# Linear attention and an ELU feed-forward layer: the second layer by seven products on all of K, exp and relu in place in G, and work placed anew on the engines

## The chip, the cores and the metric

The kernel runs on one core of a Trainium2 chip. A core has five engines that the profile names: PE (TensorE, matrix products; PEld is its loading of weights), DVE (VectorE), ACT (ScalarE), POOL (GpSimd) and SP (SyncE, which only issues DMA transfers here). The metric is the time of one execution in microseconds on the device; the time given is the median of several runs.

## The reference, cut to what matters

```python
# q, k, v: [batch 8, heads 8, seq 576, head_dim 64], f32
q_s = softmax(q, over head_dim)
k_s = softmax(k, over seq)
kv = np.einsum('bhsd,bhse->bhde', k_s, v)
attn = np.einsum('bhsd,bhde->bhse', q_s, kv)
x = attn.transpose(0, 2, 1, 3).reshape(4608, 512)
h = x @ w_in                                  # [4608, 512] @ [512, 2048]
g = np.where(h > 0, h, np.exp(np.minimum(h, 0)) - 1)
out = g @ w_out                               # [4608, 2048] @ [2048, 512]
```

## The kernel before

**Tiling.** The attention is worked in sixteen units n, one for each batch and half of its heads (two pairs of heads). A unit's q, k and v are loaded (L359); ScalarE takes the exponentials of q (L398, L428) and k (L402); VectorE sums q's over head_dim (L430) and takes the reciprocal (L433); QS (L441) is the scaled q; v is cast to bf16 in VB (L418), with a column of ones for k's sums. TensorE or a DMA transposes QS (L465, L481), TensorE makes kv (L521), VectorE or ScalarE writes it to MBLK (L530, L534), TensorE makes attn (L552, L564), and copies (L586 on ScalarE, L589 on VectorE) bring it into XT, the ring of transposed x.

The feed-forward part goes over nine blocks j of 512 tokens. The first layer of a block has eight groups g. A group (`hg_mm`, L637) is eight 128x512 matmuls, into one of the four PSUM slots of 1024 columns (blocks 2 to 8 take turns between two). Then `hg` takes exp on ScalarE (L653) into ESB, relu(1 - exp) on ScalarE in ESB (L673), and two operations of VectorE, max(h, 0) minus that, into G (L676). The even groups of blocks 0 and 1 have two operations of VectorE instead (L681, L683). G (tile GR) has 24 units of 512 columns, written and read in turn; a block fills sixteen.

The second layer reads G. K, 2048 long, is sixteen tiles of 128, in eight pairs z, which three groups hold: z 0 to 3, 4 and 5, 6 and 7. The plain way (`out_mm`, L698) takes sixteen 128x512 matmuls for 128 tokens. The other way (`pair`) works on 256 tokens, half of a block, and is a form of Strassen's method after Winograd: per z seven products of 256 columns (`mms`, L850) in the place of four of 512. It needs sums of G's quarters A11, A12, A21, A22 (`sums` and `late`, by `add_sum`, L798): four for each group of z in each pair, in place in G or into SB. It needs differences of the weights' quarters (`combos`, L769), made once, and additions of the partial results out of PSUM (`dve`, L871), with two copies for each pair (`copy`, L876). NSP = 6 holds room for six z only: blocks 2 to 5 do z 6 and 7 plainly (`std`, L863), and from block 6 on (WHOLE) TB2 and SB2, which lie where q and k were loaded before, serve the third group. Blocks 0 and 1 are plain throughout.

**What sets the order.** Each call of `S.add` records an operation with its engine, a cost and what it reads, writes or alters (R, W, X). ORDER is a list of operation numbers for each engine, written out: an engine issues in exactly that order, and `emit` puts a semaphore wait where an operation depends on another engine's. Costs, due times and DMA rates in `Sched` serve only to model the start of each operation; from it `fill` takes the number of spare matmuls (L956) that keep TensorE busy ahead of the first real ones. An operation that waits holds all that stand behind it in its engine's list. Loads are issued from SP's and GpSimd's queues (L359; W1 at L379 and W2 at L388 from GpSimd's), output stores from SP's (L731).

Of the kernel before, what the change touches and what calls it, by code (L numbers as in the profile page):

```python
# [21 lines left out]
NSP = 6  # L22
# [26 lines left out]
    "act": (  # L49
# [12 lines left out]
    "dve": (  # L62
# [35 lines left out]
}  # L98


class Op:
    __slots__ = ("eng", "dur", "emit", "deps", "key", "idx", "start", "end",
                 "dma", "sem", "val", "clock", "nbytes", "follow", "side", "late", "packet", "margin",
                 "gate", "span", "behind", "early")

    def __init__(self, eng, dur, emit, key, dma=None, nbytes=0):
        self.eng, self.dur, self.emit, self.key = eng, dur, emit, key
        self.deps = {}
        self.dma, self.nbytes = dma, nbytes
        self.start = self.end = None  # L110
        self.behind, self.early = None, 0
        self.follow, self.side, self.packet, self.margin = None, 0, 4608, 0


class Sched:
# [4 lines left out]
    LAND = 350  # L120
# [40 lines left out]
    def order(self):  # L161
# [4 lines left out]
        while any(line.values()):  # L166
            before = len(seq)
            for e in self.ENG:
                while line[e]:
                    o = line[e][0]  # L170
                    near = [d for d in (o.follow, o.gate, o.behind) if d is not None]
                    if any(d.end is None for d in list(o.deps) + near):
                        break
# [982 lines left out]
```

## Time and profile before

| what | us |
| --- | --- |
| median of three runs | 294.91 (294.35 to 295.12) |
| span of the profiled execution | 292.2 |
| clearing, loads and transposes up to the first matmul of the first layer | 14.27 |
| end of block 0's first layer | 29.91 |
| last sixteen first-layer matmuls of the last block end | 273.4 |
| idle time of VectorE ahead of L676, waiting for relu | 55.0 in 46 waits |
| idle time of ScalarE ahead of exp (L653), waiting for matmuls | 36.9 in 43 waits |
| idle time of GpSimd ahead of v casts (L418), waiting for loads | 16.1 in 5 waits |

The span is one execution as the profiler recorded it, from the first instruction to the last; the runs' times hold something more ahead and behind. In the lines of the profile, L637 is a line of the kernel, `x8` a count, `GR<-PS,ESB` reads "writes GR, reads PSUM and ESB", and the shapes are partitions x elements. "Busy" is the time that an engine is at work on instructions; the chain of waits is followed back from the last instruction to what released it at each step. The clock granted to TensorE is full in the whole span.

### The profile page before, as it was taken

What the parts mean: (1) busy time and instruction counts of PE and PEld (TensorE: products, weight loads), DVE (VectorE), ACT (ScalarE), POOL (GpSimd) and SP (SyncE); (2) the same over time, 40 slices, a digit from 0 to 9 for tenths busy, and PEclk for the clock granted to TensorE, in tenths of its full rate; (3) what the DMA queues carried; (4) which work ended last, traced back from release to release, by engine and by line L of the source; (5) the groups of instructions that cost most, each with busy time, mean ns of one, the idle gap of its engine ahead of it and who ended that gap; (6) DMA issues with size and microseconds to landing.
All of it is one profiled execution on the core that took longest, in us unless ns stands there. A gap on an engine that the chain in (4) does not pass through costs nothing.

```text
span 292.2 us, 5351 instructions
## 1 busy us (share of the span) xinstructions
PE 282.1 (97%) x2128; PEld 242.1 (83%) x2128; DVE 177.4 (61%) x326; ACT 211.3 (72%) x249; POOL 220.6 (76%) x216
## 2 busy tenths in 40 slices
PE   2899999999999999999999999999999999999994
PEld 0478887778888888888988888988989889988994
DVE  3748834787464686575656675756542667356753
ACT  4858849988998989786976779856883667665610
POOL 1992435617788999899786979799678968899880
PEclk9999999999999999999999999999999999999999
DMA  7999999799995679577919476403111010400235
GB/s 254 397 367 388 389 389 335 169 281 332 274 316 125 101 232 159 168 182 254 234 45 207 150 157 202 98 16 77 38 36 36 2 31 5 110 0 2 55 90 144
DMA packets 36472, 50.01 MB, mean 171 GB/s; under 512 B 16352, under 2 KB 18144, under 8 KB 36448
## 3 DMA queue, kind: packets, MB, share of 16 engines
q1 hardware_dynamic: 29680, 33.96, 43.5%
q0 software_dynamic: 6528, 15.47, 17.6%
q10 hardware_dynamic: 240, 0.26, 0.4%
q8 instruction: 16, 0.26, 0.4%
q14 instruction: 8, 0.07, 0.1%
HBM read 36.70 MB, written 9.44 MB: 158 GB/s over the span
## 4 chain that ended last, share of the span: by engine, by line
PE 94%; DMA 2%; POOL 2%; SPq 0%; issue 0%; DVE 0%
PE PS L637 46%; PE PS L850 28%; PE PS L698 10%; PE PS L863 5%; PE PS L552 3%; DMA KR<-in_k_dram 2%; PE PS L521 2%; POOL W L379 1%; POOL VB L418 0%; PE PS L465 0%; POOL QS L441 0%; SPq L359 0%; PE PS L564 0%; DVE OSB L871 0%
## 5 line engine op out<-in xcount | busy, mean ns | idle before, releaser
L637 PE MATMUL PS<-XT,W 128*128 128x512 f32 x576 | 142.7, 393 | 0.1
L676 DVE SCALAR_TENSOR_TENSOR GR<-PS,ESB 128x512 fp32r<-128x512 f32 (+1 forms) x124 | 87.5, 705 | 59.6 <-ACT ESB L673 55.7
L637 PEld LDWEIGHTS PS<-XT,W 128*128 128x128 f32 x576 | 105.0, 188 | 21.5 <-DMA W<-in_moe_w_in_dram 0.5
L653 ACT ACTIVATE ESB<-PS 128x1024 f32<-128x1024 f32 x72 | 73.5, 1025 | 38.4 <-PE PS L637 36.9
L673 ACT ACTIVATE ESB<-ESB 128x1024 f32<-128x1024 f32 x64 | 67.8, 1060 | 1.5
L798 POOL TENSOR_TENSOR GR<-GR 128x512 fp32r<-128x512 f32 (+1 forms) x65 | 62.7, 982 | 5.5 <-PE PS L850 4.9
L871 DVE TENSOR_TENSOR OSB<-OSB,PS 128x256 f32<-128x256 f32 x84 | 34.6, 417 | 26.9 <-PE PS L850 25.7
L850 PE MATMUL PS<-W,GR 128*128 128x256 f32 x288 | 45.5, 284 | 0.0
L850 PE MATMUL PS<-TB,GR 128*128 128x256 f32 x288 | 43.8, 283 | 0.0
L441 POOL TENSOR_TENSOR QS<-QR,RZQ 128x1152 f16<-128x1152 f32 (+1 forms) x16 | 30.2, 1886 | 17.2 <-DVE RZQ L433 16.5
L850 PEld LDWEIGHTS PS<-W,GR 128*128 128x128 f32 x288 | 40.8, 190 | 2.0
L850 PEld LDWEIGHTS PS<-TB,GR 128*128 128x128 f32 x288 | 39.9, 191 | 1.7
L798 POOL TENSOR_TENSOR SB<-GR 128x256 fp32r<-128x256 f32 (+1 forms) x31 | 30.0, 973 | 11.4 <-DVE GR L676 10.4
L698 PE MATMUL PS<-W,GR 128*128 128x512 f32 x128 | 32.4, 395 | 0.0
L798 POOL TENSOR_TENSOR GR<-SB,GR 128x256 fp32r<-128x256 f32 (+1 forms) x31 | 29.9, 978 | 2.4 <-PE PS L850 1.9
L418 POOL CAST VB<-VR 128x1152 bf16<-128x1152 f32 (+1 forms) x16 | 17.7, 1106 | 16.1 <-DMA VR<-in_v_dram 16.1
L698 PEld LDWEIGHTS PS<-W,GR 128*128 128x128 f32 x128 | 23.4, 188 | 4.7 <-DVE GR L683 0.2
L430 DVE TENSOR_REDUCE ZQ<-QR 128x18 f32<-128x1152 f32 (+2 forms) x18 | 21.8, 1209 | 6.5 <-ACT QR L428 4.9
L586 ACT ACTIVATE XT<-PS 128x512 fp32r<-128x512 f32 (+6 forms) x32 | 19.2, 603 | 6.8 <-PE PS L552 3.0
L876 ACT ACTIVATE OSB<-PS 128x256 f32<-128x256 f32 x28 | 10.4, 377 | 18.3 <-PE PS L850 9.3
L402 ACT ACTIVATE KR<-KR 128x1152 bf16<-128x1152 f32 x16 | 18.4, 1157 | 0.8 <-DMA KR<-in_k_dram 0.8
L398 ACT ACTIVATE QR<-QR 128x1152 f32<-128x1152 f32 x14 | 16.3, 1161 | 1.5 <-DMA QR<-in_q_dram 1.5
(57 smaller groups left out, 220.4 us busy)
## 6 DMA issues: line engine op xcount, KB each, us to landing
out_dram<-OSB SPq DMA_DIRECT2D x61, 128.0 KB, 2.4
QR<-in_q_dram SPq DMA_DIRECT2D x12, 576.0 KB, 5.0
KR<-in_k_dram SPq DMA_DIRECT2D x12, 576.0 KB, 6.1
VR<-in_v_dram SPq DMA_DIRECT2D x12, 576.0 KB, 5.4
W<-in_moe_w_out_dram POOLq DMA_DIRECT2D x4, 1024.0 KB, 16.6
QR<-in_q_dram POOLq DMA_DIRECT2D x4, 576.0 KB, 12.1
VR<-in_v_dram POOLq DMA_DIRECT2D x4, 576.0 KB, 13.0
KR<-in_k_dram POOLq DMA_DIRECT2D x4, 576.0 KB, 11.1
```

The costliest lines, as they stand in the source:

```text
L402: S.add("act", t_act(1152, False), lambda e: e.activation(ek[:, :, :, :].rearrange("p h c d -> p (h c d)"), flat(k), AF.Exp), key - 2, X=[ ...
L430: S.add("dve", t_dve(m), lambda e, qp=qp, zp=zp: e.tensor_reduce(zp, qp, AX.X, ALU.add), key - 3, R=[f"qR{i}{x}" for x in xs], W=[f"ZQ{i}{ ...
L441: lambda e, qp=q[:, :, a:b, :], rz=rz, dst=qs[:, :, a:b, :]: e.tensor_tensor(dst, qp, rz, ALU.mult),
L586: S.add("act", t_act((h1 - h0) * n_, True), lambda e, dst=dst, src=src: e.activation(dst, src, AF.Copy), key, W=W, X=X)
L637: last = e.matmul(P[:, t * 512:(t + 1) * 512], self.W1[:, kc, tt * 128:(tt + 1) * 128], self.XT[:, kc, rc:rc + BLK], start=(kc == 0), stop ...
L653: S.add("act", t_act(1024, True), lambda e: e.activation(esb[:, :], self.PS[ps][:, :], AF.Exp), key, W=[f"E{i}"], X=banks)
L673: S.add("act", t_act(1024, False), lambda e: e.activation(esb[:, :], esb[:, :], AF.Relu, bias=1.0, scale=-1.0), key, X=[f"E{i}"])
L676: S.add("dve", t_dve(512 if j else 1024), lambda e, u=u: e.scalar_tensor_tensor(*(x[:, :, u, :] if j else x for x in (gt, P)), 0.0, ev[:, ...
L698: last = e.matmul(dst, self.tile(jb, jj, ts), self.W2[:, jj, c0:c1], start=(jj == 0), stop=(jj == 15))
L798: lambda e: e.tensor_tensor(dst, a, b, op), key, R=R, W=W, X=X, after=after)
L850: last = e.matmul(dst, a[i][:, y_, :], b[i][:, y_, :], start=start and i == 0 and y_ == 0, stop=stop and i == len(grps) - 1 and y_ == z - ...
L871: S.add("dve", t_dve(256), lambda e: e.tensor_tensor(dst, a, b, ALU.add), key, R=R, W=W, X=X, after=after)
```

## The change

- NSP goes from 6 to 8, so that TB and SB have room for all K. Every pair takes all three groups; `std`, TB2 and SB2 are gone. T1 of the third group lies in W2 like the others.
- The later half of block 1 (two of its four pieces of 128 tokens) goes by `pair(1, 1)`, placed beside the first layer of block 2; `combos` for all three groups come ahead of it.
- ESB is gone. exp, relu and the even groups' first operation write G itself, through GE, a second name of the same memory in f32; L676's successor works on it in place.
- For casts of v, QS, the copies out of PSUM, the widening copies, the combos and the sums, the caller gives the engines that can do it, each with its cost, and `add` takes the one in whose list of ORDER the operation stands. ORDER is new on all engines. By it VectorE makes 80 sums (3 before) and GpSimd 100 (133 before), VectorE 15 of the 30 copies of 256 columns, most copies into XT, 4 of 12 combos; ScalarE 7 of the 14 full v casts.
- Instructions: TensorE 2201 (2128), of these 96 of the second layer with 512 columns (192) and 840 with 256 (672); VectorE 446 (326), ScalarE 228 (252), GpSimd 171 (216). There are 13 spare matmuls (12).
- In the new order VectorE's first q sum stands ahead of the clearing of the identity matrix, on which the spare matmuls depend, and GpSimd issues W1's third and fourth pieces behind a cast of v, a load of q and a QS. W1's groups 4 and 5 come with one load in the place of two.
- The planner's own fields (follow, gate, margin, late) are gone and its constants changed.

```diff
--- before.py
+++ after.py
-NSP = 6
+NSP = 8
...
         self.ops = []
+        self.home = {int(i): e for e, line in ORDER.items() for i in line.split()}
...
+    def add(self, eng, dur, emit, key, R=(), W=(), X=(), dma=None, nbytes=0, after=(), side=0):
+        alts = eng if isinstance(eng, dict) else {}
+        if alts:
+            eng = self.home.get(len(self.ops))
+            eng = eng if eng in alts else next(iter(alts))
+            dur = alts[eng]
         op = Op(eng, dur, emit, key, dma, nbytes)
...
+    def copy(self, e, dst, src):
+        return e.activation(dst, src, AF.Copy) if e is self.nc.scalar else e.tensor_copy(dst, src)
...
+        self.GE = nc.alloc_sbuf_tensor_at("GE", [128, 24, 2, 256], F32, offset=nc.sbuf_base - 49152)
...
-        self.ESB = [a(f"ESB{i}", [128, 1024], F32) for i in range(2)]
         self.RAW = [{t: a(f"{t.upper()}R{i}", [128, 2, CH, D], F32) for t in "qk"}
         self.VR = a("VR0", [128, 2, CH, D], F32)
-        self.TB2 = nc.alloc_sbuf_tensor_at("TB2", [128, 4, 2, 256], F32R, offset=rbase)
-        self.SB2 = nc.alloc_sbuf_tensor_at("SB2", [128, 2, 128], F32R, offset=rbase + 8192)
...
+                cost = {"act": t_act(int(576 * (h1 - h0)), False), "gp": 77 + 488 * (h1 - h0)}
...
+                cost = {"gp": m * 2.0 + 30, "dve": t_dve(m)}
+                if n in self.BYPOOL and ys == [0]:
+                    cost = {"dve": t_dve(m), "gp": m * 2.0 + 30}
                 rz = self.RZQ[i][:, :, a:b].unsqueeze(3).broadcast_to([128, 2, b - a, D])
-                S.add(eng, m * 2.0 + 30 if eng == "gp" else t_dve(m),
+                S.add(cost, None,
...
+            cost = {"act": t_act((h1 - h0) * n_, True), "dve": t_dve((h1 - h0) * n_)}
+            S.add(dict(sorted(cost.items(), reverse=e_ == "dve")), None,
+                  lambda e, dst=dst, src=src: self.copy(e, dst, src), key, W=W, X=X)
...
-        i = self.eslot % len(self.ESB)
-        self.eslot += 1
-        esb = self.ESB[i]
-        S.add("act", t_act(1024, True), lambda e: e.activation(esb[:, :], self.PS[ps][:, :], AF.Exp), key,
-              W=[f"E{i}"], X=banks)
         us = [self.unit(j, g, tp) for tp in range(2)]
         gw = sum((self.gnames(j, tp, (g,)) for tp in range(2)), [])
-        if j == 1:
-            gw += sorted(set(sum((self.early(u) for u in us), [])))
-        gt = self.GR[:, us[0]:us[1] + 1:us[1] - us[0], :, :]
+        over = sorted(set(sum((self.early(u) for u in us), []))) if j == 1 else []
+        gt, ge = [x[:, us[0]:us[1] + 1:us[1] - us[0], :, :] for x in (self.GR, self.GE)]
         if j:
-            gt = gt.rearrange("p u c t -> p c u t")
+            gt, ge = [x.rearrange("p u c t -> p c u t") for x in (gt, ge)]
             P = P[:, :].rearrange("p (c u t) -> p c u t", c=2, u=2)
-            ev = esb[:, :].rearrange("p (c u t) -> p c u t", c=2, u=2)
         else:
-            gt, P, ev = gt.rearrange("p u c t -> p (u c t)"), P[:, :], esb[:, :]
...
+            gt, ge = [x.rearrange("p u c t -> p (u c t)") for x in (gt, ge)]
+            P = P[:, :]
+        S.add("act", t_act(1024, True), lambda e: e.activation(ge, P, AF.Exp), key, W=gw + over, X=banks)
+        if how == "a":
             S.add("act", t_act(1024, False), lambda e: e.activation(
-                esb[:, :], esb[:, :], AF.Relu, bias=1.0, scale=-1.0), key, X=[f"E{i}"])
+                ge, ge, AF.Relu, bias=1.0, scale=-1.0), key, X=gw)
             for u in range(2) if j else (slice(0, 2),):
                 S.add("dve", t_dve(512 if j else 1024), lambda e, u=u: e.scalar_tensor_tensor(
-                    *(x[:, :, u, :] if j else x for x in (gt, P)), 0.0, ev[:, :, u, :] if j else ev, ALU.max, ALU.subtract), key,
-                    R=[f"E{i}"], W=self.gnames(j, u, (g,)) + (sorted(set(self.early(us[u]))) if j == 1 else []) if j else gw,
-                    X=banks)
+                    *(x[:, :, u, :] if j else x for x in (gt, P)), 0.0, ge[:, :, u, :] if j else ge,
+                    ALU.max, ALU.subtract), key, X=(self.gnames(j, u, (g,)) if j else gw) + banks)
         else:
             S.add("dve", t_dve(1024, 2), lambda e: e.tensor_scalar(
-                esb[:, :], esb[:, :], 1.0, -1.0, ALU.min, ALU.add), key, X=[f"E{i}"])
+                ge, ge, 1.0, -1.0, ALU.min, ALU.add), key, X=gw)
             S.add("dve", t_dve(1024), lambda e: e.tensor_tensor(
-                gt, ev, P, ALU.max), key,
-                R=[f"E{i}"], W=gw, X=banks)
+                gt, ge, P, ALU.max), key, X=gw + banks)
...
+        S.add({"act": t_act(512, True), "dve": t_dve(512)}, None, lambda e: self.copy(e, osb[:, :], src), key,
+              W=[f"O{i}L", f"O{i}R"], X=[f"b{bk}"])
...
-        if grp == 2:
-            T2, T3, T4, T1 = [self.TB2[:, s, :, :] for s in range(4)]
-        else:
-            z0, z1 = GROUPS[grp]
-            (T2, T3, T4), T1 = [self.TB[:, s, z0:z1, :] for s in range(3)], B12
+        z0, z1 = GROUPS[grp]
+        (T2, T3, T4), T1 = [self.TB[:, s, z0:z1, :] for s in range(3)], B12
...
-    def groups(self, j):
-        return (0, 1, 2) if j >= WHOLE else (0, 1)
+        early = [f"Ox{i}{x}" for i in range(z0 // 2, z1 // 2) for x in "LR"]
+        for s, (dst, a, b, W, R) in enumerate((
+                (T3, B22, B12, [f"T1{grp}"], self.w2(grp)),
+                (T1, B12, B11, [f"T3{grp}"] + self.w2(grp), []),
+                (T2, B22, T1, [f"T0{grp}"] + early, [f"T3{grp}"]),
+                (T4, B21, T2, [f"T2{grp}"], [f"T0{grp}"]))):
+            n_ = (z1 - z0) * 256
+            S.add({"gp": n_ * 2.34 + 30, "dve": t_dve(n_)}, None, lambda e, dst=dst, a=a, b=b: e.tensor_tensor(
+                dst, a, b, ALU.subtract), key, R=R, W=W, after=S.ops[-1:] if s == 1 else ())
...
-    def add_sum(self, grp, dst, a, b, op, key, R, W, X, after, eng="gp"):
+    def add_sum(self, grp, dst, a, b, op, key, R, W, X, after):
         z0, z1 = GROUPS[grp]
         n_ = (z1 - z0) * 128
-        self.S.add(eng, n_ * 2.4 + 60 if eng == "gp" else t_dve(n_),
+        self.S.add({"gp": n_ * 2.4 + 60, "dve": t_dve(n_)}, None,
                    lambda e: e.tensor_tensor(dst, a, b, op), key, R=R, W=W, X=X, after=after)
         return self.S.ops[-1]
...
-            self.add_sum(grp, A12, A12, A11, ALU.subtract, key, m, [], n, [],
-                         "dve" if (j, ts) == (NBLK - 1, 1) else "gp")
+            self.add_sum(grp, A12, A12, A11, ALU.subtract, key, m, [], n, [])
...
         S = self.S
         end = (j, ts) == (NBLK - 1, 1)
-        grps = self.groups(j)
-        full = 2 in grps
-        b0, b1 = (6, 7) if ts and full else (4, 5)
+        grps, tail = (0, 1, 2), j >= WHOLE
+        b0, b1 = (6, 7) if ts and tail else (4, 5)
         H = [self.bank(b)[:, c:c + 256] for c in (0, 256) for b in (b0, b1)]
-        if full:
+        if tail:
             x, y, over = 2 * ts, 2 * ts + 1, []
...
-        def std(p, jj0, jj1, stop):
...
         def copy(dst, src, W, bk):
-            S.add("act", t_act(256, True), lambda e: e.activation(dst, src, AF.Copy), key, W=W,
+            S.add({"act": t_act(256, True), "dve": t_dve(256)}, None, lambda e: self.copy(e, dst, src), key, W=W,
                   X=[f"b{bk}"])
...
         def second():
-            if not full:
-                std(0, 2 * NSP, 16, False)
+            pass
...
         def fourth():
-            if not full:
-                std(1, 2 * NSP, 16, False)
-            elif not end:
+            if not end:
                 dve(XR, XR, H[3], [], [], [f"O{x}R", f"b{b1}"])
             mms(1, H[1], A22, T4, g, 2, stop=True)
             dve(XL, XL, H[1], [], [], [f"O{x}L", f"b{b1}"])
-            if not full:
-                dve(XR, XR, H[3], [], [], [f"O{x}R", f"b{b1}"])
...
-        for g0, g1 in ((3, 4), (4, 5), (5, 6), (6, 8)):
+        for g0, g1 in ((3, 4), (4, 6), (6, 8)):
             self.load_w1(g0, g1, range(4), -30)
...
         work = [(1, ts, 4 + ts, 12, 16) for ts in range(2)]
-        for jj in (0, 8):
-            work += [(1, ts, 4 + ts % 2, jj, jj + 8) for ts in range(2, 4)]
         for j in range(2, NBLK):
             for g in range(8):
                 self.hg(j, g, g % 2, key, "a")
                 paced(8 * j + g)
                 if j == 2:
-                    if g in (1, 2, 3, 4, 5, 7):
+                    if g in (0, 1):
                         w = work.pop(0)
                         self.out_mm(*w, key)
-                        if w[4] == 16:
-                            self.out_store(w[0], w[1], w[2], key + 1)
+                        self.out_store(w[0], w[1], w[2], key + 1)
+                    if g == 1:
+                        for grp in range(3):
+                            self.combos(key, grp)
+                        self.sums(1, 1, key, (0, 1, 2))
+                        parts = self.pair(1, 1, key)
+                    if g in (3, 4, 5, 6):
+                        parts[g - 3]()
                     if g == 7:
-                        self.combos(key, 0)
-                        self.combos(key, 1)
                         self.sums(2, 0, key, (0, 1))
                 else:
                     ts, i = g // 4, g % 4
-                    if g == 0 and j - 1 >= WHOLE:
-                        if j - 1 == WHOLE:
-                            self.combos(key, 2)
+                    if g == 0:
                         self.sums(j - 1, 0, key, (2,))
                     if i == 0:
                         parts = self.pair(j - 1, ts, key)
                     parts[i]()
                     if i == 1:
                         n_ = (j - 1 + ts, 1 - ts)
-                        self.sums(*n_, key, self.groups(j - 1) if ts == 0 else (0, 1))
+                        self.sums(*n_, key, (0, 1, 2) if ts == 0 else (0, 1))
```

More of the change, by code (lines that the diff above doesn't have):

```diff
@@ L102 @@
     __slots__ = ("eng", "dur", "emit", "deps", "key", "idx", "start", "end",
-                 "dma", "sem", "val", "clock", "nbytes", "follow", "side", "late", "packet", "margin",
-                 "gate", "span", "behind", "early")
+                 "dma", "sem", "val", "clock", "nbytes", "side", "early", "alts")
     def __init__(self, eng, dur, emit, key, dma=None, nbytes=0):
@@ L110, in __init__ @@
         self.start = self.end = None
-        self.behind, self.early = None, 0
-        self.follow, self.side, self.packet, self.margin = None, 0, 4608, 0
+        self.side = self.early = 0
 class Sched:
@@ L163, in order @@
         free = {e: 740.0 for e in self.ENG}
-        queue = {e: 0.0 for e in self.ENG}
-        seq = []
+        queue, seq = 0.0, []
         while any(line.values()):
-            before = len(seq)
+            ready = []
             for e in self.ENG:
-                while line[e]:
+                if line[e] and all(d.end is not None for d in line[e][0].deps):
                     o = line[e][0]
-                    near = [d for d in (o.follow, o.gate, o.behind) if d is not None]
-                    if any(d.end is None for d in list(o.deps) + near):
-                        break
-                    t = max([free[e]] + [d.end + self.hop(d, o) for d in o.deps] +
-                            [d.start + (d.dur if d.eng == e else 0) for d in near[:2] if d is not o.behind])
-                    o.start, o.end = t, t + o.dur
-                    free[e] = o.end
-                    if o.dma:
-                        if o.behind is not None:
-                            queue[e] = max(queue[e], o.behind.end - self.LAND - o.behind.margin)
-                        queue[e] = max(t + self.FIRST[e], queue[e]) + o.nbytes / self.DMA_RATE
-                        o.end = queue[e] + self.LAND + o.margin
-                    seq.append(line[e].pop(0))
-            assert len(seq) > before
-        rank = {o: i for i, o in enumerate(seq)}
-        return self.fill(sorted(seq, key=lambda o: (o.start, rank[o])))
+                    ready.append((max([free[e]] + [d.end + self.hop(d, o) for d in o.deps]), e))
+            t, e = min(ready)
+            o = line[e].pop(0)
+            o.start, o.end = t, t + o.dur
+            free[e] = o.end
+            if o.dma:
+                queue = o.end = max(t + self.FIRST[e], queue) + o.nbytes / self.DMA_RATE
+            seq.append(o)
+        return self.fill(seq)
     def hop(self, d, o):
@@ L346, in init, with load @@
             S.add("dve", 80, lambda e, i=i: e.memset(self.VB[i][:, :, :, D:D + 1], 1.0), -88,
-                  W=[f"VBone{i}"], follow=S.ops[-1] if i else None)
+                  W=[f"VBone{i}"])
             S.add("dve", 280, lambda e, i=i: e.memset(self.MBLK[i][:, :, :].bitcast(F32), 0.0), -88,
-                  W=[f"MBLK{i}", f"MBLK{i}0", f"MBLK{i}1"], follow=S.ops[-1])
-        self.cleared = S.ops[-1]
-    def load(self, n, t, key, eng="gp", follow=None):
+                  W=[f"MBLK{i}", f"MBLK{i}0", f"MBLK{i}1"])
+    def load(self, n, t, key, eng="gp"):
         S = self.S
@@ L359, in load @@
         S.add(eng, ISSUE[eng], lambda e: e.dma_start(dst, src), key,
-              W=[name + "0", name + "1"] if t == "q" else [name], dma=f"{name}{eng}", nbytes=128 * 4608,
-              follow=follow)
-        S.ops[-1].margin = 0 if (n, t) in ((0, "q"), (1, "q")) else 300 if n < 4 else 800
+              W=[name + "0", name + "1"] if t == "q" else [name], dma=f"{name}{eng}", nbytes=128 * 4608)
     HALF = ((0, 5), (5, CH))
@@ L381, in load_w1 @@
             W=[f"W1_{g}{kc}" for g in range(g0, g1) for kc in kcs],
-            dma=f"w1{g0}{kcs[0]}", nbytes=len(kcs) * (g1 - g0) << 17, after=after, follow=self.ident)
-        self.S.ops[-1].margin = 300
+            dma=f"w1{g0}{kcs[0]}", nbytes=len(kcs) * (g1 - g0) << 17, after=after)
     def load_w2(self, s, key, after=()):
@@ L404, in stage1 @@
                 key - 2, X=[f"kR{i}"])
-            for eng, h0, h1, x in {"gp": [("gp", 0, 2, "")], "act": [("act", 0, 2, "")],
-                                   "dve": [("dve", 0, 2, "")],
-                                   "pair": [("act", 0, 5, ""), ("gp", 5, 9, "y")]}[vconv]:
+            for h0, h1, x in ((0, 5, ""), (5, 9, "y")) if vconv == "pair" else ((0, 2, ""),):
                 if vconv == "pair":
@@ L470, in tp @@
             W = [f"qsT{self.alt(n)}{x}" for x in W]
-            if eng == "act":
-                S.add("act", t_act(n_, True), lambda e, dst=dst, src=src: e.activation(
-                    dst, src, AF.Copy), key, W=W, X=X, after=after)
-            else:
-                S.add("dve", t_dve(n_), lambda e, dst=dst, src=src: e.tensor_copy(dst, src),
-                      key, W=W, X=X, after=after)
+            cost = {"act": t_act(n_, True), "dve": t_dve(n_)}
+            S.add(dict(sorted(cost.items(), reverse=eng == "dve")), None,
+                  lambda e, dst=dst, src=src: self.copy(e, dst, src), key, W=W, X=X, after=after)
     def turn(self, n, key):
@@ L758, in combos @@
         z0, z1 = GROUPS[grp]
-        if grp == 2:
-            early = [f"qR0{x}" for x in range(2)] + ["kR0"]
-        else:
-            early = [f"Ox{i}{x}" for i in range(4) for x in "LR"]
-        old, hi = [f"B{grp}"], grp == 2
-        for s, (dst, a, b, W, X, R) in enumerate((
-                (T3, B22, B12, [f"T1{grp}"] + early, [], self.w2(grp)),
-                (T1, B12, B11, [f"T3{grp}"] + [] if hi else [f"T3{grp}"] + self.w2(grp), [], []),
-                (T2, B22, T1, [f"T0{grp}"], [], [f"T3{grp}"]),
-                (T4, B21, T2, [f"T2{grp}"], [], [f"T0{grp}"]))):
-            S.add("gp", (z1 - z0) * 256 * 2.34 + 30, lambda e, dst=dst, a=a, b=b: e.tensor_tensor(
-                dst, a, b, ALU.subtract), key, R=R, W=W, X=X, after=S.ops[-1:] if s == 1 else S.r["qR00"][-1:] if hi and s == 0 else ())
-    def groups(self, j):
-        return (0, 1, 2) if j >= WHOLE else (0, 1)
+        early = [f"Ox{i}{x}" for i in range(z0 // 2, z1 // 2) for x in "LR"]
[7 more added lines that the diff above has]
+                dst, a, b, ALU.subtract), key, R=R, W=W, after=S.ops[-1:] if s == 1 else ())
     def sb(self, j, ts, grp):
@@ L805, in sums @@
             S1, N = self.sb(j, ts, grp)
-            own = [f"T1{grp}"] if grp == 2 and (j, ts) != (NBLK - 1, 1) else []
-            one = self.add_sum(grp, S1, A21, A22, ALU.add, key, h + g + own, N, [], self.summed.get(N[0], []))
+            one = self.add_sum(grp, S1, A21, A22, ALU.add, key, h + g, N, [], self.summed.get(N[0], []))
             self.third[j, ts, grp] = self.add_sum(grp, A21, A11, A21, ALU.subtract, key, m, [], h, [one])
@@ L856, in mms @@
                       R=list(names[i]) + ([f"T{wnames}{grp}"] if wnames is not None else self.w2(grp)))
-        def std(p, jj0, jj1, stop):
-            bk = (b0, b1)[p]
-            def mm(e):
-                for jj in range(jj0, jj1):
-                    last = e.matmul(self.bank(bk), self.tile(j, jj, 2 * ts + p), self.W2[:, jj, :],
-                                    start=False, stop=stop and jj == jj1 - 1, skip_group_check=True)
-                return last
-            S.add("pe", (jj1 - jj0) * t_f32r(512), mm, key, side=2, X=[f"b{bk}"],
-                  R=self.gnames(j, ts, range(jj0 // 2, jj1 // 2)) + [
-                      f"W2_{s}" for s in range(jj0 // 4, (jj1 + 3) // 4)])
         def dve(dst, a, b, R, W, X, after=()):
@@ L924, in program @@
         S = self.S
-        self.eslot = self.oslot = self.pairs = 0
+        self.oslot = self.pairs = 0
         self.where, self.summed, self.third = {}, {}, {}
@@ L951, in program @@
         self.xt(1, 0, 0, -10, XT1)
-        for o in S.ops:
-            if o.eng == "pe":
-                o.late = False
         S.spare_after = [self.ident]
```

67 lines of the change are left out of this document (14 added, 53 removed), and 136 rows, old and new, of the table ORDER.

## The prediction

> **What bounds it now.** I read the page's first part, then the chain that ended last by engine and by line (fourth part), then the chain piece by piece, the groups by form, the waits of TensorE, and last each engine's busy time in stretches of 30 us.
>
> ```profile
> PE 282.1 (97%) x2128; PEld 242.1 (83%) x2128; DVE 177.4 (61%) x326; ACT 211.3 (72%) x249; POOL 220.6 (76%) x216
> ...
> PE 94%; DMA 2%; POOL 2%; SPq 0%; issue 0%; DVE 0%
> ```
>
> TensorE is busy 97% of the 292.2 us span and is 94% of the chain, so what counts is its own work and the few places where it waits. Pieces of the chain (start, us, what) give the pitch of its matmuls:
>
> ```profile
> 54.16 2.14 PE PS L637 x8
> 59.06 3.89 PE PS L637 x16
> ...
> 79.65 3.63 PE PS L698 x16
> ...
> 92.91 1.85 PE PS L637 x8
> ...
> 234.62 1.91 PE PS L850 x16
> ```
>
> A 512-wide matmul takes 3.63/16 = 0.2269 us, a 256-wide one 1.91/16 = 0.1194. Eight first-layer matmuls should take 1.82. At 54.16 they take 2.14, and the sixteen at 59.06 take 3.89 instead of 3.63: 0.32 + 0.26 us of gap in block 1. There two uses of a PSUM slot are only 3.53 to 3.63 us of matmuls apart (the recorded order walked with these pitches). How soon a slot comes free again, the time line shows (start, us, engine, line), here for a group of block 6 whose matmuls end at 201.16:
>
> ```profile
> 201.20 1.03 ACT L653 ACTIVATE ESB<-PS 128x1024 f32<-128x1024 f32 x1 [0.67 <-PE PS L637]
> 202.26 1.06 ACT L673 ACTIVATE ESB<-ESB 128x1024 f32<-128x1024 f32 x1
> ...
> 203.61 1.41 DVE L676 SCALAR_TENSOR_TENSOR GR<-PS,ESB 128x512 fp32r<-128x512 f32 x2
> ```
>
> It is free at 203.61 + 1.41 = 205.02, 3.86 us after the group's end; without the L871 that stood ahead of L676 it would be 202.26 + 1.06 + 1.41 - 201.16 = 3.57. What TensorE was seen to wait for:
>
> ```profile
> PE PS L956 <- ACT QR L428: 5.6, 1, 5.6
> PE PS L564 <- DVE MBLK L534: 0.5, 1, 0.5
> PE PS L465 <- POOL QS L441: 0.2, 1, 0.2
> PE PS L521 <- POOL VB L418: 0.2, 1, 0.2
> ```
>
> The first is the start, before any input has landed. Nothing else is long: the other engines are hidden now. How far, the groups show (count, then busy us, mean ns), and the stretches (each engine's busy us of 180):
>
> ```profile
> L676 DVE SCALAR_TENSOR_TENSOR GR<-PS,ESB 128x512 fp32r<-128x512 f32 x120 | 82.6, 689 | 58.9 <-ACT ESB L673 55.0 <-PE PS L850 2.0
> L798 DVE TENSOR_TENSOR GR<-GR 128x512 fp32r<-128x512 f32 x1 | 0.9, 919 | 0.0
> L798 DVE TENSOR_TENSOR GR<-GR 128x256 fp32r<-128x256 f32 x2 | 0.8, 459 | 0.4 <-PE PS L850 0.4
> L798 POOL TENSOR_TENSOR GR<-GR 128x512 fp32r<-128x512 f32 x27 | 35.0, 1299 | 4.5 <-PE PS L850 4.3
> L418 POOL CAST VB<-VR 128x1152 bf16<-128x1152 f32 x14 | 16.1, 1149 | 16.1 <-DMA VR<-in_v_dram 16.1
> L876 ACT ACTIVATE OSB<-PS 128x256 f32<-128x256 f32 x28 | 10.4, 377 | 18.3 <-PE PS L850 9.3 <-DMA out_dram<-OSB 5.9 <-PE PS L863 3.0
> ```
>
> ```profile
> sum 180.00, PE 180.00 PEld 160.80 DVE 108.94 ACT 129.39 POOL 156.26; mean PE 30.00 PEld 26.80 DVE 18.16 ACT 21.56 POOL 26.04
> ```
>
> From 100 to 280 us TensorE has no idle time; VectorE is 61% busy, ScalarE 72%, GpSimd 87%.
>
> **The products.** Before, blocks 2 to 5 (eight pairs) run seven products on twelve of sixteen K tiles and the rest plainly (L863), and block 1 is plain. Now all K of blocks 2 to 5 and block 1's later half go by seven products. That removes 64 matmuls of L863 and 32 of L698, and adds 168 of 256 columns (eight pairs x 14, one x 56). -96 x 0.2269 = -21.78; +168 x 0.1194 = +20.06; **-1.7 us**. The pieces of four L863 matmuls take 0.91 to 0.93 rather than 0.908, over sixteen pieces at most -0.35 more: from -1.7 to -2.1, I take -1.9. All of it is on the chain.
>
> The Trainium skill, page "TensorE: Matmul & The Clock Gate", section "Back-to-back issue gap", puts the gap of a single warm matmul at N/2.4 ns plus about 2.5, which is 215.8 and 109.2 ns; the sum by it would be -2.4, an estimate, but the rows show 226.9 and 119.4, about 10 ns more each, and the measurement decides.
>
> **The gaps in block 1.** In the new order the least distance of two uses of a slot is 3.96 to 4.07 us, over the 3.86. Both gaps can go: 0 to -0.6, I take -0.3, since other places, about a dozen of 64 groups, now stand within 0.1 to 0.45 us of it.
>
> **In place in G.** ESB falls away and exp (L653) must wait until the old contents of G have been read, which only L676 waited for before. Walking the new TensorE order, the last reader ends 2.5 us or more ahead of the group's own last matmul; cost 0. If that cover were gone, exp, and with it the slot, would be late by what is lacking.
>
> **The sums.** One pair has twelve (four for each of three groups) where it had eight: 15 x 12 = 180 against 136. GpSimd keeps 100 of 133, VectorE goes from 3 to 80 (30 of 512 columns, 50 of 256). No trace shows many of these on VectorE; its three, at the end, bound them: a 512 one 0.919 with GpSimd at work beside it, and 0.689 if it went as fast as L676's; a 256 one 0.501 beside GpSimd and 0.417 alone. So 30 x 0.689 + 50 x 0.417 = 41.5 to 30 x 0.919 + 50 x 0.501 = 52.6 us. VectorE also gets half of the 30 copies out of PSUM and most copies into XT (at L589's 425 to 692 ns, 18.6 in all), four weight combinations (3.8), one QS (2.1) and six adds of L871 (2.5): 177.4 + 27.0 + 41.5 to 52.6 - 1.8 for the three it had = 244 to 255 us, 84 to 88% of the span. GpSimd falls to about 171, ScalarE to about 200. VectorE's work of two L676 is what frees a slot; one sum ahead of them makes it late by up to 0.9 us, against margins of 0.1 to 0.45. Bounds of this: 0 (all sums fall in idle time, of which VectorE keeps 37 to 48 us) to +6.6 (GpSimd is at work 60% of the time, and takes 0.230 from each of the 30 and 0.084 from each of the 50, which is 11.1; 6.6 is 60% of it, all on the chain). A dozen tight places at some 0.07 us, the part of a delay that passes a margin, give **+0.8**, nearer to the lower end because the long trace rows show idle time before L676 in 46 of its waits.
>
> The Trainium skill, "GPSIMD Engine Reference", section 1, says that VectorE and GpSimd share their SBUF interface and contend when VectorE reads two operands from SBUF; the rows agree (501 against 417 ns), and this speaks against the change, for these sums are of that kind while L676 has one operand in PSUM.
>
> **Casts and stores.** Seven of fourteen v casts go to ScalarE, about 1.15 us each, and ScalarE is in order: a cast that waits for its v load holds the next exp. GpSimd waited 16.1 us for such loads before, hidden. The v loads land 4.2 to 6.1 us after issue by stretch. Bound 0 to +6, I take 0 as likeliest: about 28 PSUM copies left ScalarE, so that it keeps 30% idle. The copies on VectorE also take on part of the 5.9 us that L876 waited for stores to land.
>
> **The start.** VectorE makes its first q reduce ahead of the clearing of the identity, so the spare matmuls begin about 6.95 us rather than 5.58; GpSimd issues W1's third and fourth pieces behind a v cast, a q load and a QS, some 12.4 and 14.0 rather than 10.26 and 10.96. Walked by rows the first layer begins at 14.85 (14.27 before) and block 0's ends at 30.1 +/- 0.6 (29.91). From -0.3 to +1.6, I take +0.2. The last block is as it was.
>
> **Sum.** -1.9 - 0.3 + 0.8 + 0.2 = -1.2. The profiled span of 292.2 becomes 291.0; the median of the runs is 294.91, 2.7 above the span, and 291.0 + 2.7 = **293.7 us**.
>
> **Rivals.** *A, the gain alone*: no new wait, from -1.9 to -2.1 - 0.3 = -2.4: 292.5 to 293.0. For it: VectorE idles before L676 for a relu, 55.0 us in all. Against: the dozen tight places. *B, VectorE becomes the bound*: it ends slower. The two-operand sums run at the contended price and stand between a relu and its L676; the slots come late and TensorE waits through blocks 2 to 8. The other terms make -1.9 - 0.3 + 0.2 = -2.0. Full price: 294.91 - 2.0 + 6.6 = 299.5; at 60% of it 296.9. It decides once more than 2.9 us (44%) reach TensorE. For it: 84 to 88% busy, with the second L676 last in each release. Against: nothing on VectorE was ever late so far. *C, ScalarE held by a late v load*: a third of the 6 us bound gives 294.91 - 2.0 + 2.0 = 294.9, no change. *D, the start slips whole*: 294.91 - 1.9 - 0.3 + 0.8 + 1.6 = 295.1, no change. That the change doesn't do what it says is excluded: the counts of instructions are 2201 on TensorE, 840 of 256 columns.
>
> **Chances.** Forecast 0.33 and A 0.17; B 0.30; C and D together 0.20. What a measurement of this kernel tells from no change is about 0.3%, 0.88 us: faster lies under 294.03, slower over 295.79. Faster gets the forecast and A but for 0.02 at its slow edge, 0.48; slower gets B and 0.03 of C and D, 0.33; the rest, 0.19, is no change. The likeliest's own range is 291.6 to 294.2; for 8 in 10 it goes from 291.6 up through C and D to B at a good half of its price, 297.2.
>
> **What would show it.** In the profile after: TensorE's busy time lower by 1.5 to 2; block 1's pieces at 1.82 to 1.85 for eight; VectorE at 84 to 88% with 512 sums near 0.92 if contended; TensorE waits on L676 of 1 us or less in all for the forecast, 3 or more for B; waits of exp on ScalarE behind a v cast for C; the first layer's end of block 0 after 30.7 for D. I am wrong if TensorE's idle time grows by over 2 us, or if the pitch of its 256-wide matmuls is not 0.119.

## The result and the profile after

The changed kernel takes 296.73 us, median of 22 runs, beside 295.04 for the kernel before: ratio 1.0062 (95% interval 1.0042 to 1.0082), **slower by 0.6%**. Forecast was 293.7, faster. The profiled execution spans 294.8 us (292.2 before). That is 2.6 us more, where the medians differ by 1.7: the execution profiled before was a short one (spans of the same kernel in later runs are 292.6 to 293.7 us at the median of each chip), so what follows accounts for two executions.

The page's busy times and the chain by engine, and what TensorE waited for the most behind the start (total us, times, longest):

```profile
PE 279.6 (95%) x2201; PEld 244.4 (83%) x2201; DVE 237.4 (81%) x446; ACT 204.4 (69%) x225; POOL 174.0 (59%) x169
...
PE 81%; DMA 8%; POOL 3%; SPq 2%; issue 2%; ACT 1%; DVE 1%; POOLq 0%
```

```profile
PE PS L797 <- ACT OSB L276: 1.7, 2, 1.2
PE PS L664 <- DVE GR L644: 1.7, 1, 1.7
...
PE PS L617 <- DMA W<-in_moe_w_in_dram: 0.4, 1, 0.4
```

Before, the chain was 94% TensorE and 2% DMA; now it is 81% and 8%. Pieces of it (start, us):

```profile
15.22 8.02 DMA W<-in_moe_w_in_dram
23.38 7.51 PE PS L617 x32
51.31 3.63 PE PS L617 x16
67.52 5.05 DMA out_dram<-OSBX
81.70 1.91 PE PS L797 x16
161.49 5.14 DMA out_dram<-OSB
```

Three transfers that were not on the path before (of W1, out of OSBX and out of OSB) stand on it now. The products are as forecast: 3.63/16 and 1.91/16, 0.2269 and 0.1194 us each.

**The wait at 76 us** is read on VectorE, and GpSimd beside it (start, us, engine, line, idle before):

```profile
72.31 0.26 DVE L420 RECIPROCAL RZQ<-ZQ 128x18 f32<-128x18 f32 x1
73.60 1.72 DVE L724 TENSOR_TENSOR TB<-W 128x512 fp32r<-128x512 f32 x1 [1.04 <-issue]
75.24 2.00 DVE L644 SCALAR_TENSOR_TENSOR GR<-PS,GE 128x512 fp32r<-128x512 f32 x3
```

```profile
72.64 2.12 POOL L430 TENSOR_TENSOR QS<-QR,RZQ 128x1152 f16<-128x1152 f32 x1 [4.20 <-DVE RZQ L420]
```

L724 makes a weight difference into TB, whose memory was OSBX until block 0's output had been stored. SP's queue had issued that store behind a transpose and loads. The last piece that L724 needs was issued at 67.52 and landed 6.0 us later, at 73.52. (The chain's piece ends at 72.57 only because VectorE's earlier work ended there; the 1.04 us of "issue" are the wait for the landing. In s2, the same stage of a kernel of the next section, the profile names it.)

```profile
74.99 1.34 DVE L725 TENSOR_TENSOR TB<-W 128x512 fp32r<-128x512 f32 x1 [1.41 <-DMA out_dram<-OSBX]
```

So the store held VectorE for 1.0 us. Then L724 took 1.72 us beside GpSimd's QS, which had begun before it, where it takes 0.63 when it begins first (below): 1.1 more. Block 1's last L644 stood behind both. TensorE's matmul starts, less the pitch, show 1.84 us of gap here.

**The waits at 166 and 171 us** are read on ScalarE:

```profile
166.65 0.38 ACT L276 ACTIVATE OSB<-PS 128x256 f32<-128x256 f32 x1 [2.32 <-DMA out_dram<-OSB]
166.93 1.16 ACT L276 ACTIVATE qsT<-QT 128x1152 fp32r<-128x1152 f16 x1
```

The copy that frees a PSUM bank for the next product waits for OSB's store to land; what was pushed back with it delays the next copy. The gaps are 1.33 and 0.71 us. That store's data lay ready at 156.6 with those of its twin, but SP issued it at 161.49 (not at 160.9, as the expectation of s2 has it), behind two loads and two later stores.

The accounts: -1.7 for products, -0.6 for block 1's two gaps, +0.6 for W1, +1.84, +2.04, and +0.6 because the first layer begins at 14.88 rather than 14.27, make +2.8 against the spans' +2.6.

### The profile page after: what moved, and what is told of

Read it like the earlier page. It is cut to its first block, busy times and chain, and to the rows that moved or that the text cites. A ratio compares the mean times of both kernels' runs of the same rounds, so it can differ in the third digit from the quotient of the medians.

```text
span 294.8 us, 5547 instructions
## 1 busy us (share of the span) xinstructions
PE 279.6 (95%) x2201; PEld 244.4 (83%) x2201; DVE 237.4 (81%) x446; ACT 204.4 (69%) x225; POOL 174.0 (59%) x169
## 4 chain that ended last, share of the span: by engine, by line
PE 81%; DMA 8%; POOL 3%; SPq 2%; issue 2%; ACT 1%; DVE 1%; POOLq 0%
PE PS L617 37%; PE PS L797 33%; PE PS L664 6%; DMA W<-in_moe_w_in_dram 3%; PE PS L535 2%; DMA KR<-in_k_dram 2%; DMA out_dram<-OSB 2%; DMA out_dram<-OSBX 2%; PE PS L504 1%; POOL QS L430 1%; SPq L693 1%; SPq L356 1%; POOL W L374 1%; POOL VB L276 1%; DVE TB L724 1%
## 5 line engine op out<-in xcount | busy, mean ns | idle before, releaser
L639 ACT ACTIVATE GE<-PS 128x1024 f32<-128x1024 f32 x72 | 73.5, 1024 | 54.3 <-PE PS L617 45.1
L644 DVE SCALAR_TENSOR_TENSOR GR<-PS,GE 128x512 fp32r<-128x512 f32 (+1 forms) x124 | 87.1, 704 | 23.4 <-ACT GE L641 21.9
L748 POOL TENSOR_TENSOR GR<-GR 128x256 fp32r<-128x256 f32 (+1 forms) x55 | 53.4, 984 | 38.1 <-DVE SB L748 29.1
L641 ACT ACTIVATE GE<-GE 128x1024 f32<-128x1024 f32 x64 | 67.9, 1061 | 1.8
L797 PE MATMUL PS<-W,GR 128*128 128x256 f32 x360 | 56.8, 283 | 1.7 <-ACT OSB L276 1.7
L797 PE MATMUL PS<-TB,GR 128*128 128x256 f32 x360 | 54.0, 283 | 0.0
L748 POOL TENSOR_TENSOR SB<-GR 128x256 fp32r<-128x256 f32 (+1 forms) x20 | 19.9, 1000 | 22.0 <-DVE GR L644 21.3
L748 DVE TENSOR_TENSOR GR<-GR 128x256 fp32r<-128x256 f32 (+1 forms) x35 | 20.2, 596 | 0.6 <-PE PS L797 0.5
L276 POOL CAST qsT<-QT 128x1152 fp32r<-128x1152 f16 x10 | 11.5, 1149 | 10.7 <-PE PS L535 8.5
L797 PE MATMUL PS<-W,SB 128*128 128x256 f32 x112 | 17.3, 283 | 0.0
```

Of the source, the lines that this page charges most:

```text
L639: S.add("act", t_act(1024, True), lambda e: e.activation(ge, P, AF.Exp), key, W=gw + over, X=banks)
L641: S.add("act", t_act(1024, False), lambda e: e.activation(ge, ge, AF.Relu, bias=1.0, scale=-1.0), key, X=gw)
L644: S.add("dve", t_dve(512 if j else 1024), lambda e, u=u: e.scalar_tensor_tensor(*(x[:, :, u, :] if j else x for x in (gt, P)), 0.0, ge[:, ...
L748: lambda e: e.tensor_tensor(dst, a, b, op), key, R=R, W=W, X=X, after=after)
L797: last = e.matmul(dst, a[i][:, y_, :], b[i][:, y_, :], start=start and i == 0 and y_ == 0, stop=stop and i == len(grps) - 1 and y_ == z - ...
```

## The experiments

All keep the computation; all but one line of code are moves in ORDER. Ratios are to the kernel before on the same chip. In moved kernels line numbers are one higher. Two accounts are set against one another: late transfers, and VectorE as the bound.

**1. Single causes put right.** s1: block 0's stores ahead in SP's list. s2: the twin store of block 3. s3: the start. s4: all three.

```diff
 s1, sp
-13 203 205 208 218 227 234 217 228 186 182 188 179 185 237 183 189 180 300
+13 186 182 188 179 185 183 189 180 203 205 208 218 227 234 217 228 237 300
 s2, sp
-750 641 778 767 766 751 642
+750 751 641 778 767 766 642
 s3, gp (67: load of unit 2's q; 16 to 20: W1); act 39 37 -> 37 39, 113 behind 111; dve 116 117 behind 112
-22 67 47 16 38 17 18 19 20 68
+22 47 16 38 17 18 19 20 67 68
```

> The changed kernel, but SP issues the eight stores of block 0's output (out of OSBX, which lies in the memory of TB) ahead of the transpose of unit 4 and the loads behind which they stood. Theory of the late transfers: the weight difference on VectorE no longer waits for the landing at 72.6 us, TensorE's wait of 1.7 to 1.8 us for L644 at 76 us is gone, and nothing else comes in its place: 296.7 - 1.8 = 294.9 us, ratio to the kernel before about 1.000. Theory of VectorE as the bound (its work of 237 us and the contention with GpSimd): the wait moves to the next L644, and the time stays at 296.2 to 296.9, ratio 1.004 to 1.007.

> The changed kernel, but the second store of one output piece of block 3 (issued at 160.9 us, though its data were there with the first's at 156.6) is issued right behind the first. Theory of the late transfers: the copy out of PSUM on ScalarE no longer waits for this landing, the gaps of TensorE at 166 and 171 us (1.3 and 0.7) are gone: 296.7 - 2.0 = 294.7 us, ratio about 0.999. Theory of VectorE as the bound: not over 0.5 us gained, ratio 1.004 to 1.007.

> The changed kernel with two orders of the start put back: GpSimd issues the load of unit 2's q behind all pieces of W1 (its exponential and sum stand behind those of the first layer's sixth group again), and ScalarE takes unit 1's exponential of k ahead of its cast of v. Theory of the late transfers: the wait for W1 at 23 us (0.6) goes and the first layer begins some 0.3 to 0.5 earlier: 296.7 - 0.9 = 295.8 us, ratio 1.003. Theory of VectorE as the bound: what is gained at the start is lost in block 1, ratio 1.005 to 1.007.

> All three edits of order in one kernel; the products, the sums, their engines and VectorE's load are those of the changed kernel. Theory of the late transfers: the three gains add, 1.8 + 2.0 + 0.9 = 4.7 from 296.7: 292.0 us, ratio 0.990, faster than both kernels. Theory of VectorE as the bound: not under 295.0, ratio 1.000 or more.

Measured: s1 1.0070 (1.0030 to 1.0109); s2 **0.9984** (0.9956 to 1.0013), 294.32 us; s3 1.0118 (1.0070 to 1.0165); s4 1.0109 (1.0062 to 1.0157). s2 is as the theory of late transfers has it: both gaps are gone from its profile, though the one at 76 us is there (2.0 us). s1 took away the store wait, and the difference itself is short; it began 0.17 us ahead of QS:

```profile
74.14 0.63 DVE L725 TENSOR_TENSOR TB<-W 128x512 fp32r<-128x512 f32 x1
```

but nothing is gained: TensorE waits at 56, 70 and 86 us instead (0.8, 1.0 and 0.9), as a megabyte of stores now runs ahead of the loads. The chain goes through these (start, us):

```profile
57.93 7.88 DMA KR<-in_k_dram
...
80.21 5.53 DMA out_dram<-OSB
```

s3 moved too much: unit 2's q came so late that its transposes waited (1.0 us for QS at 34 us), and another 0.7 went at 46 us, where a copy into XT and W2 came late; at W1 it gained 0.3. s4 has these waits too, and others at 59, 74 and 90 us. So late transfers are a cause, but not ones that can be moved ahead of one another freely.

**2. The difference put later on VectorE.** t1 does that alone, t2 with s2's store, t3 also with W1's groups 4 and 5 by two loads, t4 also with `37 39` on ScalarE and the second MBLK cleared behind QS on VectorE.

```diff
 t1, dve (351: the difference; 287 288, 294 295: L644)
-350 298 351 287 288 294 240 295 241
+350 298 287 288 294 240 295 351 241
 t3
-        for g0, g1 in ((3, 4), (4, 6), (6, 8)):
+        for g0, g1 in ((3, 4), (4, 5), (5, 6), (6, 8)):
```

> The changed kernel, but VectorE makes the weight difference that waits for the store out of OSBX (middle group, L724 into TB) four operations of L644 later; no transfer and no other queue is altered. If what cost 1.8 us at 76 us was only that L644 stood behind this wait: 296.7 - 1.8 = 294.9 us, ratio about 1.000. If, as the moved stores showed, late loads of k and v in that stage take its place: the next wait comes from them, and 296.0 to 296.7, ratio 1.003 to 1.007, is left.

> That edit together with the moved store of block 3 (which alone gave 294.3 us). If the two waits are independent: 294.3 - 1.8 = 292.5 us, ratio 0.992. If the transfers of block 1's stage bound it anyway: 293.8 to 294.3, ratio 0.997 to 0.999. If VectorE's load were the bound, a new wait of TensorE for L644 would be seen in blocks 2 to 7.

> Those two edits, and W1's groups 4 and 5 by two loads again, as before the change: the first half has only 0.5 MB of its own ahead of it. If the wait for W1 at 23 us (0.4 in one profile, 1.0 in another) is the load's size: 0.4 to 1.0 us less than without, 291.5 to 292.1, ratio 0.988 to 0.991. If it is the order of the loads ahead of it (q of unit 2 before the last pieces): no change, 292.5.

> Those three, and at the start ScalarE takes unit 1's exponential of k ahead of its cast of v, and VectorE clears the second MBLK behind unit 1's QS rather than ahead of it. If the later begin of the first layer (14.9 to 15.2 us against 14.3) comes from these two: 0.3 to 0.5 us less, ratio 0.987 to 0.990. If it comes from the late identity matrix and the spare matmuls: no change.

Measured: t1 1.0078 (1.0044 to 1.0113), t2 1.0040 (1.0012 to 1.0067), t3 1.0015 (0.9989 to 1.0042), t4 1.0080 (1.0053 to 1.0107). The gap at 76 us is gone and more than that comes between 80 and 105 us (waits of TensorE in t1):

```profile
PE PS L618 <- DVE GR L645: 1.2, 2, 1.0
PE PS L798 <- DVE OSB L277: 1.0, 1, 1.0
PE PS L798 <- DVE OSB L807: 0.4, 1, 0.4
```

Two things are at work. VectorE is full at first, as the slower rival had it for blocks 2 to 8: it is busy 9.71 of the 10 us from 80 on in t2, where TensorE has gaps of 0.5 and 0.4. But TensorE's longest wait, 1.6 us at 94 us in t2 and t3, goes back along the chain to a load of k that landed at 89.87; ScalarE stood before its exponential, and the next exp and relu behind it, late loads as t1's expectation had them:

```profile
89.89 1.17 ACT L397 ACTIVATE KR<-KR 128x1152 bf16<-128x1152 f32 x1 [1.92 <-DMA KR<-in_k_dram]
```

Ahead of the last of these gaps, of 0.6 us at 102, a sum of 0.69 us alone was held 2.63 while GpSimd made a QS:

```profile
96.96 2.63 DVE L749 TENSOR_TENSOR SB<-GR 128x512 fp32r<-128x512 f32 x1
```

```profile
96.92 2.13 POOL L431 TENSOR_TENSOR QS<-QR,RZQ 128x1152 f16<-128x1152 f32 x1
```

(the first from VectorE's, the second from GpSimd's time line of t2). QS ends at 99.05, and the sum 0.54 us later, its own time. The same in the changed kernel at 73.60: QS runs from 72.64 to 74.76, L724 ends at 75.32. t4's two moves at the start gained nothing: the first layer begins at 15.21 (15.40 in t3), but W1 is waited for again, 0.6 us at 27 us.

**3. The two differences on GpSimd**, in gaps that it has there. u5: that alone. u1: with s2's store. u2: also with W1's two loads. u3: u2 with the identity cleared first (its kernel has W1's two loads, other than its expectation says).

```diff
 u5, dve
-346 350 298 351 287
+346 298 287
 u5, gp
-236 299 361
+236 350 299 351 361
 u3, dve (numbers from 20 on are one higher with the added load)
-25 0 6
+0 26 6
```

> The changed kernel, but GpSimd makes the two weight differences of the middle group that VectorE made between 71 and 75 us (T1 into W, and T2 into TB, which waits for the store out of OSBX), in gaps of 4.2 and 2.0 us that GpSimd has there; no transfer is moved. If VectorE, in line behind the store and slowed by GpSimd (1.72 us where it takes 0.6 alone), is what makes TensorE wait at 76 us and full in the 30 us after it: the wait goes and none comes in its place, 296.7 - 1.8 = 294.9, ratio 1.000. If the loads of this stage bind anyway, as in the kernel with all stores first: 296 or more, ratio 1.004 to 1.007.

> The same together with the moved store of block 3. If each of the two is a cause of its own: 294.3 - 1.8 = 292.5 us, ratio 0.991 to 0.993, faster than both kernels. If VectorE is full from 76 to 105 us all the same: 294 or more, ratio 0.998 to 1.004, with a new wait of TensorE for VectorE between 80 and 105 us.

> Those two, and W1's groups 4 and 5 by two loads, as before the change. The wait for W1 at 23 us was 0.4 and 1.0 us in two profiles of the one order and none with the split: 0.4 to 1.0 less than without, ratio 0.988 to 0.991, if nothing takes it back.

> The two edits for stores and weight differences without the split, and VectorE clears the identity matrix first, so that GpSimd and the spare matmuls need not wait for the first sum of q. If the late identity is why the first layer begins at 14.9 to 15.2 us rather than 14.3: up to 0.6 us less than without, ratio 0.989 to 0.991. If the begin hangs on unit 1's QS and exponential of k: no change.

Measured: u5 1.0045 (1.0016 to 1.0074), u1 0.9977 (0.9957 to 0.9997), u2 **0.9964** (0.9937 to 0.9990), 293.68 us, u3 0.9970 (0.9959 to 0.9982). In u5 and u1 the gap at 76 us is gone, and a copy that waits for a store 10 us later takes 0.8 to 1.0 of it back; so u1 is no better than s2, and u5 not clearly better than the changed kernel. u1 and u5 differ by the moved store alone: 2.1 us of the medians (t2 and t1, in the same way, by 1.1). In u2 hardly a wait is left:

```profile
PE PS L455 <- DVE QS L431: 0.7, 1, 0.7
PE PS L798 <- POOL W L725: 0.2, 1, 0.2
```

Its span is 291.0 us, 1.2 under the kernel before's, with a first layer that begins 0.7 later (14.96): nearly all of the products' gain. By the medians u2 is 0.4 us faster than u1, which the intervals don't part. In u3 the first layer begins 0.3 earlier (14.66), but W2 is waited for, 0.6 us at 45 us, and the time is as in u2.

**4. Beside one another, and all that helped.** v0 is the changed kernel, v2 is s2 again, v1 is the same kernel as u3.

> The changed kernel as it is, beside the three others on the same chip: 296.5 us, ratio 1.004 to 1.008, with TensorE's gaps at 76 us and at 166 and 171 us again. If those were accidents of one execution, they are not in this profile.

> The changed kernel with the one moved store of block 3 again (294.3 us, ratio 0.998 before), beside the changed kernel itself: 2.0 us less than that if the store is a cause in every execution; less than 1 us if the landing is late in some only.

> All edits that helped: the moved store, the middle group's two weight differences on GpSimd, W1's groups 4 and 5 by two loads, the identity first. If the late transfers and VectorE's place in line behind one of them were all that the products' gain was lost to: 293.0 us, ratio 0.992 to 0.996, with no gap of TensorE over 0.5 us from 24 us on. If start and loads trade against one another (with the identity first, W2 came 0.6 late): 293.7, as with either of the two alone.

Measured: v0 1.0043 (1.0011 to 1.0076), 296.80 us; v2 0.9974 (0.9943 to 1.0006), 294.59; v1 **0.9954** (0.9927 to 0.9982), 294.18. In v0 the gap at 76 us is back at 1.85, again with a stretched difference, 2.37 us (73.03 to 75.40, QS from 72.73 to 74.85); those at 168 and 172 are 0.39 and 0.71. So both recur, with sizes that follow the landing. But the one at 76 us does not come in every execution of this order: in v2, whose kernel is that of s2, the store landed at 73.21, VectorE reached the difference 0.17 us ahead of GpSimd's QS, and TensorE has no gap there:

```profile
73.33 0.65 DVE L725 TENSOR_TENSOR TB<-W 128x512 fp32r<-128x512 f32 x1
```

```profile
73.50 2.47 POOL L431 TENSOR_TENSOR QS<-QR,RZQ 128x1152 f16<-128x1152 f32 x1 [4.18 <-DVE RZQ L421]
```

It waits 1.2 us at 86 us instead. The moved store is worth 2.2 us of the medians. v1 beats the kernel before by 0.2 to 0.7%, and the changed kernel by 2.6 us of the medians. W1 was waited for again,

```profile
PE PS L618 <- DMA W<-in_moe_w_in_dram: 1.6, 1, 1.6
```

where u3's profile, of the same kernel, shows no wait for W1: that wait differs from one execution to the next.

## Why the prediction was wrong

- **Products** (-1.9): right in pitch and count; -1.7.
- **Block 1's gaps** (-0.3): both went, -0.6.
- **In place** (0): no wait of TensorE. The cover was misread, though: in three groups (first of block 6, fifth of blocks 7 and 8) the last reader of the old G stands 0.72 us behind the group's last matmul, not 2.5 ahead. By the trace exp then started about 0.7 late, and TensorE shows no gap behind it.
- **Sums** (+0.8; up to +6.6): VectorE's sums took 46.7 us, inside 41.5 to 52.6, and VectorE 237.4, under the 244 forecast. That forecast added durations to a busy time: the durations of VectorE's instructions grew by 73.6 us, inside what was added (66.7 to 77.8), but its busy time by 60.0, since consecutive records overlap by some 0.1 us at their ends. From 100 us on, apart from the store's gaps, TensorE shows no more idle time than before, although VectorE is 82 to 91% busy. Rows of VectorE after:

```profile
L748 DVE TENSOR_TENSOR GR<-GR 128x512 fp32r<-128x512 f32 x14 | 10.8, 774 | 0.1
L748 DVE TENSOR_TENSOR GR<-GR 128x256 fp32r<-128x256 f32 x21 | 9.9, 477 | 0.5 <-PE PS L797 0.5
```

  So the slower rival did not hold for blocks 2 to 8. VectorE cost time in one stage, block 1's end and block 2, through the moved weight differences, which the forecast priced at 3.8 us of busy time in all and for which it named no wait. The measured time lies close to that rival's 296.9, but by another mechanism; that is chance.
- **Casts and stores** (0): **this is the step that failed.** It looked at v loads, which cost nothing (ScalarE waited 5.0 us for them, TensorE never). Stores it dismissed in a sentence, though the row of L876 showed 5.9 us of waits for landings in six places; these were hidden, and the plain matmuls that the change removed (0.9 us in each half of a pair) may have been part of the cover; no run puts them back. Nor did it ask what else needs OSBX's memory: the differences that were needed at block 6 for the third group, and at the end of block 2 for the others, were brought forward to 71 us while SP's list kept the stores back until 64.75. Of the 3.9 us that stores cost in the account, the 2.04 of block 3's are shown by the runs: moving that one store gave 1.1, 2.1 and 2.2 us of the medians, each on one chip. The 1.84 at 76 us are read off the trace; three edits that take this wait away (s1, t1, u5) did not make the kernel clearly faster, as other waits took its place.
- **The start** (+0.2): +1.2 in this profile, 0.6 late, as the forecast's own walk had it (14.85 against 14.88 measured), and 0.6 waiting for W1, within the bounds stated; taken far too low. Block 0's first layer ends at 30.89, past the 30.7 that was named as the sign of D. What makes the wait for W1 stays open: with the load in one piece it is between nothing (s1) and 1.2 us (s2), with two loads nothing in t3, u2 and u3, but 0.6 in t4 and 1.7 in v1.

Of the signs named for being wrong, TensorE's idle time did grow by over 2 us, and the pitch held. The step from span to time was off as well: 2.7 us were added, and for the profiled run after it is 1.85.

Open: why the copy at 86 us waits in u1, u5 and v2 but not in u2, u3 and v1; the one difference in their code that goes with it is W1's two loads.

The Trainium skill's page "GPSIMD Engine Reference", section 1, has VectorE and GpSimd contend when VectorE reads two operands from SBUF. The three held operations agree (1.72, 2.37 and 2.63 us beside a QS that began first, where two that began ahead of theirs took 0.63 and 0.65), and go further than the 501 against 417 ns that the forecast took for the price.

## What to carry to other kernels

When work is brought forward, follow every buffer it writes back to the last transfer out of it, and that transfer back through its queue: a store that nobody waited for can stand behind loads until somebody does. Matmuls that a change removes may also have been the time in which copies and stores were hidden; take the landing rows of the removed stage and ask which of them still fit. And before an operation goes to an engine because that has idle time over the span, look at the busy time of the stage it goes to, at what it would run beside there, and at which of the two begins first. Before a wait of a microsecond is given a cause, look for it in a second profile of the same kernel.

## What the runs showed of the hardware

Of a VectorE operation on two SBUF operands and GpSimd's QS (128x1152), the one that began first ran at its own speed and the other was held. With QS first (2.12 to 2.13 us), the operation of 0.63 to 0.69 us ended some 0.55 us after QS did, in the changed kernel, v0, s2, s3, t2 and t3. With the difference first, by 0.17 us, it took 0.63 to 0.65 and QS 2.45 to 2.47, in s1, s4 and v2: QS lost some 0.33 of the 0.47 us that they overlapped. Beside GpSimd's sums the slowing was less, to 774 ns on average against 0.68 to 0.69 alone.

The pieces of 128 KB that leave the chip landed in 2.4 us at the median, but block 3's late one in 5.1 and the eight out of OSBX, with loads of 576 KB issued around them, in 5.0 to 7.5.

In v0 the clock granted to TensorE was 0.54 from 76.1 to 79.7 us, right behind the gap, and its 512-wide matmuls started 0.427 us apart; in the changed kernel's first profile, behind the same gap, it was 1.00.
